# Chunk 1's feature tiles 4 to 7 as seven block products, with chunk 0 run through to its end before chunk 1

## The chip, the cores and the metric

The kernel runs on one core of a Trainium2 chip. The metric is the device time of the whole program in microseconds (us). The time before the change is 263.39 us, the median of three runs (263.13 to 263.56).

## What is computed

An attention block with polynomial sketches is followed by a two-layer network with exact GELU. Cut to what matters:

```python
# q, k, v: (4 batches, 4 heads, 1088 tokens, 32);  S1, S2: (8, 32)
phi(x)[i, j] = (S1 x)[i] * (S2 x)[j]                # 64 features of each token
kv = sum over tokens of phi(k) v^T;  z = sum over tokens of phi(k)
attn = phi(q) kv / (phi(q) z + 1e-6)
x = attn as (4352 tokens, 128)
h = x @ w_in                                         # w_in: 128 x 2048
out = (0.5 * h * (1 + erf(h / sqrt(2)))) @ w_out     # w_out: 2048 x 128
```

The weights arrive as 64-bit numbers. The kernel turns them into 32-bit ones on the chip ("rounding": five instructions on VectorE or GpSimd and two on ScalarE for each piece of weights).

## The kernel before

**Tiling.** The 4352 tokens are cut into eight chunks of 512 tokens (two for each batch) and a ninth for the remainders. The 2048 hidden columns are sixteen feature tiles of 128, called fi. For each chunk n and each fi, `hidden(n, fi)` (matmuls at L683, GELU by ScalarE at L690) computes 128 features by 512 tokens. The result then has to be multiplied by its 128 rows of `w_out` and added up over fi.

**Two ways of the second product.** In the usual way, `project(n, fi)` (L818) is one 128x128 by 512 matmul that adds into one PSUM bank, `o_of[n]`. In the other way, four feature tiles make a block (b = fi // 4), and each pair of them is multiplied as a 2 by 2 block matrix with seven products in place of eight. This needs sums of features, `token_sums(n, b)`: four GpSimd instructions of 128x512 (L732 to L735). It also needs sums of weights, `channel_sums(i)`: four GpSimd instructions (L719 to L722) for weight piece i. A call of `two_products` (L767) issues two products of 64x256 that run side by side in the two column halves of TensorE; a block has seven such calls. They add into two PSUM banks, `acc[n]`, which `drain(n)` (ScalarE L779 to L781, VectorE L783 to L788) and `combine(n)` put together. Where a chunk used both ways, `take_usual(n)` (ScalarE, L795) has copied the usual part out of PSUM, and `combine` adds it.

Before the change, chunks 0 and 1 run fi 0 to 7 in the usual way (`USUAL = 8`) and fi 8 to 15 as blocks 2 and 3. All later chunks run blocks 0 to 3. The last, the ninth, is done in the usual way.

**Order.** Every engine runs its instructions in the order of the program text, and the text is written step by step: step t does `hidden` of entry t of the list `steps`, then everything that `at(t, ...)` has put into slot t, then the second products put into `products[t]`. Before the change, `steps` runs chunk 0 fi 0-3, chunk 1 fi 0-3, chunk 0 fi 4-7, chunk 1 fi 4-7, chunk 0 fi 8-15 (steps 16 to 23), chunk 1 fi 8-15 (steps 24 to 31), and from step 32 the whole of chunk 2, and so on. A usual product stands two steps behind its hidden tile (`LAG = 2`). Seven-product calls stand three to six steps behind the last hidden tile of their block.

**What shares those steps.** The weights lie in five pieces: fi 0-1, 2-3, 4-7, 8-11 and 12-15. `round_at(t, ...)` spreads the rounding of a piece over steps t and t + 1: `w_in_sb[2]` at 4, `w_out_sb[2]` at 6, `w_in_sb[3]` at 8, `w_out_sb[3]` at 10, `w_in_sb[4]` at 12 and `w_out_sb[4]` at 14. The last multiplication of the two pieces 4 is done by GpSimd (L297), the others by VectorE. `channel_sums(3)` is put at step 13 and `widen_v_rem(1)` (L349 and L351, a memset and a copy that reads values brought by DMA) at step 12. Batch 1's keys (`features_of_all`, L934; `outer_of_all`, L942 to L949; `turn_keys_rem`, L333; `add_tokens`, L958; `finish_keys`, L428; `turn_kv`, L458; `z_sum`) fill steps 16 to 23. The factors of chunk 2's queries (`query_sketch`, L568; `query_outer`, L580 to L603) come at step 24. At step 28 VectorE turns batch 2's keys (`key_turn_blocks`, L359). At step 31 TensorE does `sketch_and_attend(3)` (L568, then L617) and `features_of_all(2)` (L934, which reads the turned keys).

Buffers: `hps` (the hidden tiles) has two banks, so that `hidden` of step t waits for the GELU of step t - 2. `ops` has two banks. `block` tiles have three buffers.

Of the kernel before, what the change touches and what calls it, by code (L numbers as in the profile page):

```python
# [16 lines left out]
def kernel(  # L17
# [24 lines left out]
    NF = d_ff // 128  # L42
# [7 lines left out]
    NCH = J // JC  # L50
    C = D + 1
    LAG = 2
    NMAIN = B * NCH
    NB = 4

    USUAL = 8
    NCHUNK = NMAIN + 1
    assert B == 4 and d_model == 128 == H * D == JC * D == 2 * F and H == 4 and REM == 64 and NCH == 2

# [7 lines left out]
    def work_banks():  # L67

        return wps.tile([128, 2, CW], FP, name="w_ps")

    def work_bank():
        return work_banks()[:, 0]

    def halves(banks):
        return [banks[:, i] for i in range(2)]

    def hidden_bank():
        return hps.tile([128, CW], FP, name="h_ps")

    def out_bank():  # L80
        return ops.tile([128, CW], FP, name="o_ps")
# [55 lines left out]
    def block(dtype=U32):  # L137

        b = big.tile([128, NB, 512], U32, name="block", bufs=3)
        return b if dtype == U32 else b.bitcast(dtype)  # L140
# [314 lines left out]
    def turn_kv(b, banks):  # L455

        for rows in (slice(0, 64), slice(64, 128)):
            pe.matmul(banks[rows, 1, :128], lhsT=kv_T[b], rhs=ident, start=True, stop=True)  # L458
        act.copy(out=kz[b], in_=banks[:, 1, :128])
# [200 lines left out]
    def turn_half(n, i, ps, copy):  # L660
        if i == 0:
            xT[n] = att.tile([128, CW], FP, name="xT", bufs=3)
        for j in range(2):
            pe.transpose(ps[:, j * 128:(j + 1) * 128], in_=x_tok[n, i][:, j].rearrange("p h d -> p (h d)"), identity=ident)
        copy(out=xT[n][:, i * 256:(i + 1) * 256], in_=ps[:, :256])
# [4 lines left out]
    def w_tile(w, fi):  # L670
        i = max(i for i, (c0, c1) in enumerate(pieces) if c0 <= fi * 128)
        at = fi * 128 - CUTS[i]
        return w[i][:, at:at + 128]
# [3 lines left out]
    def hidden(n, fi, by_halves=False):  # L677
        W = width[n]
        ps = first_banks.pop((n, fi)) if (n, fi) in first_banks else hidden_bank()
        w = w_tile(w_in_sb, fi)  # L680
        for rows in (slice(0, 64), slice(64, 128)) if by_halves else (slice(0, 128),):
            if (n, fi) not in begun:
                pe.matmul(ps[rows, :W], lhsT=w[:, rows], rhs=xT[n][:, :W], start=True, stop=True)  # L683
        if n < NCH and fi < USUAL:
            g_of[n, fi] = mlp.tile([128, CW], FP, name="g", bufs=4)
        else:
            if fi % NB == 0:
                blocks[n, fi // NB] = block(FP)
            g_of[n, fi] = blocks[n, fi // NB][:, fi % NB]
        act.activation(out=g_of[n, fi][:, :W], in_=ps[:, :W], func=ACT.Gelu)  # L690
# [58 lines left out]
        return sums[n, b][j][:, e], T[j][:, k]  # L749

    def first_block(n):
        return USUAL // NB if n < NCH else 0

    def two_products(n, b, i):

# [37 lines left out]
    def take_usual(n):  # L793
        usual[n] = mlp.tile([128, CW], FP, name="g", bufs=4)
        act.copy(out=usual[n], in_=o_of[n])  # L795
# [9 lines left out]
        return N[:, 1]  # L805

    def project(n, fi, parts=range(B // 2)):
        first, final = fi == 0, fi == (USUAL if n < NCH else NF) - 1
        if first:
            o_of[n] = out_bank() if n < NMAIN else [work_bank() for i in range(B // 2)]  # L810
        g = g_of[n, fi]
        if n == NMAIN:

            for i in parts:
                pe.matmul(o_of[n][i][:, :128], lhsT=g[:, i * 128:(i + 1) * 128], rhs=w_tile(w_out_sb, fi),  # L815
                          start=first, stop=final)
            return
        pe.matmul(o_of[n], lhsT=w_tile(w_out_sb, fi), rhs=g, start=first, stop=final)  # L818
# [65 lines left out]
    late = []  # L884
# [32 lines left out]
    w_out[0].fields()  # L917


    steps = [(n, fi) for f in range(0, USUAL, 4) for n in range(NCH) for fi in range(f, f + 4)]  # L920
    steps += [(n, fi) for n in range(NCHUNK) for fi in range(USUAL if n < NCH else 0, NF)]
    slots = {t: [] for t in range(len(steps) + LAG)}

    def at(t, f, *a):
        slots[t].append(lambda: f(*a))
# [40 lines left out]
    held = {}  # L966
# [21 lines left out]
    def round_at(t, w, product_by=dve):  # L988
        r = []
        at(t, lambda: (r.append(Rounding(w)), r[0].low_words(), r[0].fields()))  # L990
        at(t + 1, lambda: (r[0].exponents(), r[0].mantissas(), r[0].signs(), r[0].product(product_by)))
# [2 lines left out]
        round_at(t0, w_in_sb[i + 2])  # L994
        round_at(t1, w_out_sb[i + 2])
    round_at(12, w_in_sb[4], pool)
    at(13, channel_sums, 3)

    at(12, widen_v_rem, 1)
    for r in range(2):  # L1000
        at(14, key_turn_blocks, 1, r)
    round_at(14, w_out_sb[4], pool)
    at(15, query_turn, 2)
    at(16, features_of_all, 1)
    at(16, outer_of_all, 1)
    at(16, turn_keys_rem, 1)
    at(17, features_rem, 1)
    at(17, add_tokens, 1)
    at(18, channel_sums, 4)

    at(21, finish_keys, 1, False)
    at(22, lambda: turn_kv(1, held["kv"]))
    at(23, z_sum, 1)
    at(23, fold_z, 1)
    at(23, query_turn, 3)
    at(24, query_sketch, 2)
    at(24, query_outer, 2)
    for i, t in enumerate((25, 26, 28)):
        at(t, channel_sums, i)
    at(11, spread_sketches)  # L1020
    at(40, repeat_first_z)
    for n in range(3, NCHUNK):

        t = (n - 1) * NF
# [28 lines left out]
    products = {t: [] for t in range(len(steps) + LAG)}  # L1053
    done = {t: [] for t in range(len(steps) + LAG + 1)}
    drains = {t: [] for t in range(len(steps) + LAG + 1)}
    for t, (n, fi) in enumerate(steps):
        if n < NCH and fi < USUAL:
            products[t + LAG].append((project, n, fi))
            if fi == USUAL - 1:
                slots[t + LAG + 1 + 2 * n].append(lambda n=n: take_usual(n))  # L1060
        elif n == NMAIN:
            at_ = max(t + LAG, (n * NF + 5) if fi < 3 else (n * NF + 6) if fi < 5 else 0)
            if fi < NF - 4:
                products[at_].append((project, n, fi))
            if fi == NF - 1:

                products[at_] += [(project, n, NF - f, (i,)) for f, i in ((4, 0), (3, 0), (2, 0), (4, 1), (1, 0), (3, 1),
                                                                          (2, 1), (1, 1))]
                done[at_ + 1].append(n)
        elif fi % NB == NB - 1:  # L1070
            b = fi // NB
            opens = b == first_block(n)
            late = int(n < NCH or n == NCH and opens)
            for later, pairs in ((3, 3), (4, 2), (5, 2)) if opens else ((2, 2), (3, 2), (4, 1), (5, 2)):
                later += late
                for i in range(pairs):
                    products[t + later].append((two_products, n, b, len([p for q in products.values() for p in q
                                                                        if p[:3] == (two_products, n, b)])))
            if b == NF // NB - 1:
                drains[t + 6 + late].append(n)  # L1080
                done[t + 12].append(n)

    for t in range(len(steps) + LAG):
        if t < 4:

            hidden(0, t)
            if t == 1:
                w_out[0].low_words()
                w_out[0].exponents()
                w_out[0].finish()  # L1090
                w_out[1].fields()
            if t == 2:
                w_out[1].low_words()
            if t == 3:
                banks = work_banks()
                numerators_by_token(1, halves(banks), range(JC))
                w_out[1].mantissas(by_pool=True)
                w_out[1].exponents()
                divide(1, banks, range(JC), by_head_pair=False)
                w_out[1].signs()  # L1100
                w_out[1].product()
                for u in range(4):
                    for f, *a in products[u]:
                        f(*a)
            continue
        if t == 4:
            for i, copy in enumerate((by_act, by_dve)):
                turn_half(1, i, work_bank(), copy)
            first_hidden(1, 0)
            for f, *a in products[t]:  # L1110
                f(*a)
            first_hidden(1, 1)
        for n in drains[t]:
            drain(n)
        if t < len(steps):
            n, fi = steps[t]
            hidden(n, fi, by_halves=t >= 18 and (n < NMAIN or fi < 5))
        if t < len(steps) and steps[t][0] < NMAIN and steps[t][1] % NB == NB - 1:
            n, b = steps[t][0], steps[t][1] // NB
            if b >= first_block(n):  # L1120
                token_sums(n, b)
        for f in slots[t]:
            f()
        for n in done[t]:
            store(n)
        if t != 4:
            for f, *a in products[t]:
                f(*a)
# [41 lines left out]
```

## Time and profile before

| | |
|---|---|
| median of three runs | 263.39 us (263.13 to 263.56) |
| the profiled execution: time | 263.46 us |
| the profiled execution: span | 261.7 us (1.8 us lie around it) |
| TensorE (PE) busy | 256.7 us, 98% of the span |
| VectorE (DVE) busy | 150.7 us, 58% |
| ScalarE (ACT) busy | 116.6 us, 45% |
| GpSimd (POOL) busy | 164.0 us, 63% |
| granted TensorE clock | 1.00 throughout |

The busy shares are means over the span; a page of the profile also divides it into forty slices. PE is full in nearly all slices. POOL is nearly idle from about 23 to 39 us and nearly full from 50 to 75 us; DVE is nearly full from 30 to 55 us. A line of the timeline gives the start and the duration in us, the engine, the line of the kernel, and output <- inputs. On TensorE, one 32-bit matmul stands as two records ("x2"), and the durations of consecutive records overlap, so the distance from start to start tells what a matmul takes from the engine.

### The profile page before, as it was taken

How to read it: one execution, taken by the hardware profiler on the slowest of the kernel's cores; microseconds unless marked ns; L12 is line 12 of the kernel's file. 1: busy time of each engine (PE TensorE's matmuls, PEld its weight loads, DVE VectorE, ACT ScalarE, POOL GpSimd, SP SyncE). 2: the span in 40 equal slices, each digit the busy share in tenths (PEclk: the TensorE clock that was granted, in tenths of full speed). 3: DMA queues.
4: the chain of work that ended last, by engine and by line, in shares of the span. 5: the costliest groups of instructions: out<-in, count | busy, mean ns of one | idle time of the engine just before them, and what ended most of it. 6: DMA issues, size and time to landing. Idle time of an engine off the chain costs nothing.

```text
span 261.7 us, 5752 instructions
## 1 busy us (share of the span) xinstructions
PE 256.7 (98%) x2331; PEld 132.7 (51%) x2331; DVE 150.7 (58%) x307; ACT 116.6 (45%) x227; POOL 164.0 (63%) x173
## 2 busy tenths in 40 slices
PE   8999999999999999999999999999999999999994
PEld 6845444344444454444444454454444444445794
DVE  2885879969697997590267948450646042600240
ACT  4674767532635334533335334533362335334441
POOL 3403007799968767687758766967778676877200
PEclk9999999999999999999999999999999999999999
DMA  6469848831000101002000020010000100010020
GB/s 200 139 200 357 164 107 206 214 81 15 3 0 15 28 4 30 10 3 40 3 0 3 0 33 11 3 30 10 3 0 14 30 4 0 14 28 0 3 40 20
DMA packets 29530, 13.48 MB, mean 52 GB/s; under 512 B 21824, under 2 KB 27712, under 8 KB 29504
## 3 DMA queue, kind: packets, MB, share of 16 engines
q1 hardware_dynamic: 29472, 13.12, 20.5%
q8 instruction: 18, 0.29, 0.5%
q14 instruction: 8, 0.07, 0.1%
q10 hardware_dynamic: 32, 0.00, 0.0%
HBM read 10.88 MB, written 2.23 MB: 50 GB/s over the span
## 4 chain that ended last, share of the span: by engine, by line
PE 96%; DVE 1%; ACT 1%; issue 0%; DVEq 0%
PE h_ps L683 44%; PE o_ps L767 33%; PE o_ps L818 5%; PE w_ps L815 3%; PE w_ps L428 1%; PE w_ps L617 1%; PE w_ps L568 1%; PE w_ps L848 1%; PE h_ps L697 1%; PE o_ps L417 1%; PE h_ps L333 1%; PE w_ps L934 1%; PE w_ps L635 0%; PE w_ps L534 0%; DVE x_tok L656 0%
## 5 line engine op out<-in xcount | busy, mean ns | idle before, releaser
L683 PE MATMUL h_ps<-xT,w_in 128*64 128x512 f32 (+3 forms) x514 | 137.3, 576 | 0.0
L690 ACT ACTIVATE block<-h_ps 128x512 f32<-128x512 f32 (+1 forms) x128 | 73.0, 570 | 120.4 <-PE h_ps L683 114.6
L767 PE MATMUL o_ps<-block,w_out 128*64 128x256 f32 x224 | 57.9, 381 | 0.3 <-DVE sums L788 0.3
L683 PEld LDWEIGHTS h_ps<-xT,w_in 128*64 128x64 f32 (+1 forms) x514 | 41.8, 143 | 29.5 <-issue 11.6
L732 POOL TENSOR_TENSOR bits_low<-block 128x512 f32<-128x512 f32 x28 | 35.6, 1273 | 28.7 <-ACT block L690 28.7
L767 PEld LDWEIGHTS o_ps<-block,w_out 128*64 128x64 f32 x224 | 30.1, 137 | 39.3 <-issue 25.3
L733 POOL TENSOR_TENSOR bits_a<-block 128x512 f32<-128x512 f32 x28 | 35.7, 1276 | 13.4 <-ACT block L690 13.4
L734 POOL TENSOR_TENSOR bits_e<-bits_a,block 128x512 f32<-128x512 f32 x28 | 36.3, 1298 | 2.2
L735 POOL TENSOR_TENSOR bits_m<-block,bits_e 128x512 f32<-128x512 f32 x28 | 35.8, 1279 | 2.2
L767 PE MATMUL o_ps<-bits_low,small 128*64 128x256 f32 x112 | 29.3, 384 | 0.0
L767 PE MATMUL o_ps<-block,small 128*64 128x256 f32 x112 | 29.3, 384 | 0.0
L767 PE MATMUL o_ps<-bits_a,small 128*64 128x256 f32 x112 | 29.1, 383 | 0.0
L783 DVE TENSOR_TENSOR sums<-o_ps,sums 64x512 f32<-64x512 f32 x8 | 5.5, 682 | 41.1 <-ACT sums L780 23.6
L767 PE MATMUL o_ps<-bits_m,w_out 128*64 128x256 f32 x112 | 28.8, 380 | 0.0
L580 DVE STREAM_TRANSPOSE w_ps<-w_ps 128x512 f32<-128x512 f32 (+1 forms) x7 | 4.8, 691 | 38.8 <-PE w_ps L568 27.8
L767 PEld LDWEIGHTS o_ps<-block,small 128*64 128x64 f32 x112 | 14.5, 137 | 18.8 <-issue 9.1
L767 PE MATMUL o_ps<-bits_e,small 128*64 128x256 f32 x112 | 17.2, 385 | 0.0
L818 PE MATMUL o_ps<-g,w_out 128*128 128x512 f32 x32 | 16.4, 598 | 0.0
L767 PEld LDWEIGHTS o_ps<-bits_m,w_out 128*64 128x64 f32 x112 | 15.4, 137 | 0.0
L767 PEld LDWEIGHTS o_ps<-bits_a,small 128*64 128x64 f32 x112 | 14.7, 137 | 0.0
L767 PEld LDWEIGHTS o_ps<-bits_low,small 128*64 128x64 f32 x112 | 14.6, 137 | 0.0
L767 PEld LDWEIGHTS o_ps<-bits_e,small 128*64 128x64 f32 x112 | 7.5, 137 | 10.5 <-issue 9.1
(181 smaller groups left out, 300.6 us busy)
## 6 DMA issues: line engine op xcount, KB each, us to landing
out_dram<-oT SPq DMA_DIRECT2D x26, 64.0 KB, 2.2
block<-in_moe_w_in_dram SPq DMA_DIRECT2D x3, 512.0 KB, 7.4
block<-in_moe_w_out_dram SPq DMA_DIRECT2D x3, 512.0 KB, 12.7
k<-in_k_dram SPq DMA_DIRECT2D x12, 128.0 KB, 3.2
v<-in_v_dram SPq DMA_DIRECT2D x12, 128.0 KB, 3.4
q<-in_q_dram SPq DMA_DIRECT2D x24, 64.0 KB, 2.3
k<-in_k_dram SPq DMA_DIRECT2D x2, 256.0 KB, 2.9
q<-in_q_dram SPq DMA_DIRECT2D x2, 256.0 KB, 4.4
```

Of the source, the lines that this page charges most:

```text
L333: pe.transpose(ps[:, i * 128:(i + 1) * 128], in_=s, identity=ident)
L580: dve.transpose(out=tok, in_=ps[:, :, :H2])
L683: pe.matmul(ps[rows, :W], lhsT=w[:, rows], rhs=xT[n][:, :W], start=True, stop=True)
L690: act.activation(out=g_of[n, fi][:, :W], in_=ps[:, :W], func=ACT.Gelu)
L732: pool.tensor_sub(out=s[3], in0=a11, in1=a21)
L733: pool.tensor_add(out=s[1], in0=a21, in1=a22)
L734: pool.tensor_sub(out=s[2], in0=s[1], in1=a11)
L735: pool.tensor_sub(out=s[4], in0=a12, in1=s[2])
L767: pe.matmul(acc[n][bank][half * 64:(half + 1) * 64, col:col + HW], lhsT=fixed, rhs=moving, start=opens and e == 0 and name in "4715", stop ...
L783: dve.tensor_add(out=C[lo, 1], in0=a1[lo], in1=C[lo, 0])
L815: pe.matmul(o_of[n][i][:, :128], lhsT=g[:, i * 128:(i + 1) * 128], rhs=w_tile(w_out_sb, fi), start=first, stop=final)
L818: pe.matmul(o_of[n], lhsT=w_tile(w_out_sb, fi), rhs=g, start=first, stop=final)
```

## The change

Chunk 1 now runs only fi 0 to 3 in the usual way; its fi 4 to 7 become a block of seven products (block 1), as its blocks 2 and 3 already are. The order of the steps becomes: chunk 0 fi 0-3, chunk 1 fi 0-3, chunk 0 fi 4-15 (steps 8 to 19), chunk 1 fi 4-15 (steps 20 to 31). From step 32 on nothing changes. Chunk 0's usual products for fi 5, 6 and 7 are spread to steps 12, 14 and 16. `channel_sums(2)`, which chunk 1's block 1 needs, moves from step 28 to step 9, and `channel_sums(3)` from step 13 to step 12. Batch 1's keys move by two steps or one, and chunk 2's sketch from step 24 to step 26. `hidden` is written as two column halves from step 17 on, before from step 18.

```diff
-    USUAL = 8
+    USUAL = [8, 4]
...
-        if n < NCH and fi < USUAL:
+        if n < NCH and fi < USUAL[n]:
...
-    steps = [(n, fi) for f in range(0, USUAL, 4) for n in range(NCH) for fi in range(f, f + 4)]
-    steps += [(n, fi) for n in range(NCHUNK) for fi in range(USUAL if n < NCH else 0, NF)]
+    steps = [(n, fi) for n in range(NCH) for fi in range(4)]
+    steps += [(n, fi) for n in range(NCHUNK) for fi in range(4 if n < NCH else 0, NF)]
...
     round_at(12, w_in_sb[4], pool)
-    at(13, channel_sums, 3)
+    at(9, channel_sums, 2)
+    at(12, channel_sums, 3)
 
     at(12, widen_v_rem, 1)
...
-    at(16, features_of_all, 1)
-    at(16, outer_of_all, 1)
-    at(16, turn_keys_rem, 1)
-    at(17, features_rem, 1)
-    at(17, add_tokens, 1)
+    at(18, features_of_all, 1)
+    at(18, outer_of_all, 1)
+    at(18, turn_keys_rem, 1)
+    at(19, features_rem, 1)
+    at(19, add_tokens, 1)
     at(18, channel_sums, 4)
 
-    at(21, finish_keys, 1, False)
-    at(22, lambda: turn_kv(1, held["kv"]))
-    at(23, z_sum, 1)
-    at(23, fold_z, 1)
-    at(23, query_turn, 3)
-    at(24, query_sketch, 2)
-    at(24, query_outer, 2)
-    for i, t in enumerate((25, 26, 28)):
+    at(22, finish_keys, 1, False)
+    at(23, lambda: turn_kv(1, held["kv"]))
+    at(24, z_sum, 1)
+    at(24, fold_z, 1)
+    at(24, query_turn, 3)
+    at(26, query_sketch, 2)
+    at(26, query_outer, 2)
+    for i, t in enumerate((25, 26)):
         at(t, channel_sums, i)
...
-        if n < NCH and fi < USUAL:
-            products[t + LAG].append((project, n, fi))
-            if fi == USUAL - 1:
-                slots[t + LAG + 1 + 2 * n].append(lambda n=n: take_usual(n))
+        if n < NCH and fi < USUAL[n]:
+            to = t + LAG + max(fi - NB, 0)
+            products[to].append((project, n, fi))
+            if fi == USUAL[n] - 1:
+                slots[to + 1 + 2 * n].append(lambda n=n: take_usual(n))
...
-            late = int(n < NCH or n == NCH and opens)
+            late = int(n < NCH or n == NCH and opens) + int(n == 0 and opens)
...
-            hidden(n, fi, by_halves=t >= 18 and (n < NMAIN or fi < 5))
+            hidden(n, fi, by_halves=t >= 17 and (n < NMAIN or fi < 5))
```

(`USUAL` becomes `USUAL[n]` also in `first_block` and `project`.)

More of the change, by code (lines that the diff above doesn't have):

```diff
@@ L751, in first_block @@
     def first_block(n):
-        return USUAL // NB if n < NCH else 0
+        return USUAL[n] // NB if n < NCH else 0
     def two_products(n, b, i):
@@ L807, in project @@
     def project(n, fi, parts=range(B // 2)):
-        first, final = fi == 0, fi == (USUAL if n < NCH else NF) - 1
+        first, final = fi == 0, fi == (USUAL[n] if n < NCH else NF) - 1
         if first:
```

## The prediction

> **What bounds the kernel now.** I read the page's busy shares first, then its chain, then the engines' timelines over the stretch that the change reorders.
>
> ```profile
> PE 256.7 (98%) x2331; PEld 132.7 (51%) x2331; DVE 150.7 (58%) x307; ACT 116.6 (45%) x227; POOL 164.0 (63%) x173
> ...
> PE 96%; DVE 1%; ACT 1%; issue 0%; DVEq 0%
> ```
>
> TensorE is busy for 98% of the span and is 96% of the chain that ended last. Work taken from TensorE shortens the run, and whatever makes it wait lengthens it by the full wait, because nothing later has room to take it up. TensorE's timeline gives the two prices, from start to start:
>
> ```profile
> 39.05 1.02 PE L818 MATMUL o_ps<-g,w_out 128*128 128x512 f32 x2
> 39.90 1.02 PE L683 MATMUL h_ps<-xT,w_in 128*128 128x512 f32 x2
> ...
> 77.78 0.38 PE L767 MATMUL o_ps<-block,w_out 128*64 128x256 f32 x1
> 77.79 0.38 PE L767 MATMUL o_ps<-bits_a,small 128*64 128x256 f32 x1
> ...
> 78.65 1.03 PE L683 MATMUL h_ps<-xT,w_in 128*64 128x512 f32 x4
> ```
>
> A usual product takes 39.90 - 39.05 = 0.86, and so does a hidden tile. Two calls of `two_products` stand between 77.78 and 78.65 (each call is two passes of two records), so a call takes 0.43. In the reordered stretch TensorE runs at this pace without a gap. GpSimd and VectorE do not:
>
> ```profile
> 39.31 0.77 POOL L351 COPY v_rem_aug<-v_rem 64x128 f32<-64x128 f32 x1 [16.12 <-DMA v_rem<-in_v_dram]
> 41.26 1.28 POOL L297 TENSOR_TENSOR w_in<-bits_m,bits_e 128x512 f32<-128x512 f32 x1 [1.17 <-DVE bits_e L292]
> 42.49 0.66 POOL L719 TENSOR_TENSOR small<-w_out 128x128 f32<-128x128 f32 x1
> ...
> 44.69 0.78 POOL L722 TENSOR_TENSOR small<-w_out,small 128x128 f32<-128x128 f32 x1
> 45.44 1.26 POOL L297 TENSOR_TENSOR w_out<-bits_m,bits_e 128x512 f32<-128x512 f32 x1
> 46.78 0.46 POOL L719 TENSOR_TENSOR small<-w_out 128x128 f32<-128x128 f32 x1
> ```
>
> ```profile
> 37.77 0.69 DVE L297 TENSOR_TENSOR w_out<-bits_m,bits_e 128x512 f32<-128x512 f32 x1
> 38.38 0.42 DVE L268 TENSOR_SCALAR bits_e<-block 128x512 uint32<-128x512 uint32 x1
> ...
> 40.48 0.69 DVE L292 SCALAR_TENSOR_TENSOR bits_e<-block,bits_r 128x512 uint32<-128x512 uint32 x1 [0.55 <-ACT bits_r L279]
> ```
>
> The reader is to see when `w_in_sb[4]`, the weights of fi 12 to 15, is finished: GpSimd multiplies it from 41.26 to 42.5. Before, its first reader is `hidden` of step 20, near 49.7, seven us later. `channel_sums(3)` comes after it, at 42.49, and takes 2.95 (to 45.44) beside VectorE's rounding; the next four of the same size take 1.8 (46.78 to 48.59).
>
> **What the Trainium skill says.** Perfetto Trace Analysis, section Identifying the Most-Contended Engine, warns that matmul busy time is no good measure of the distance from the peak[...]. The trace agrees (records of 1.02 that start 0.86 apart), so I use start-to-start distances. SBUF — State Buffer, section Who interferes with whom: a VectorE instruction with two SBUF inputs, or in a two-port mode, contends with GpSimd reads. The trace agrees: L719 took 0.66 and 0.46. TensorE: Matmul & The Clock Gate, section Architectural detail, calls GpSimd's queue strictly first in, first out. The trace agrees: behind L351, which sat 16.12 for a DMA, nothing else ran.
>
> **The change part by part.**
>
> *Work.* Four usual products leave (4 x 0.86 = 3.44), seven calls come (7 x 0.43 = 3.01): -0.43 on TensorE. Four token sums are added on GpSimd (4 x about 1.28 = 5.1); GpSimd's backlog from 50 us is dealt with below. ScalarE has the same number of GELUs and copies, VectorE and all DMA issues are the same; SP's queue does not change, so `v_rem` still lands at 39.3.
>
> *The deadline of `w_in_sb[4]`.* Up to step 11 nothing moves on TensorE (its hidden tile starts at 34.75 in both orders). Afterwards chunk 0's products are thinned out: steps 11, 13 and 15 have a hidden tile alone, steps 12 and 14 also a usual product. So steps 11 to 15 hold five hidden tiles and two usual products, 7 x 0.86 = 6.01, and step 16 comes at 40.76. It is now chunk 0's fi 12: the first reader of `w_in_sb[4]`.
>
> *When `w_in_sb[4]` is ready.* Its rounding keeps its steps. But in GpSimd's queue `channel_sums(3)` now stands ahead of `widen_v_rem(1)` and of the multiplication. It needs `w_out_sb[3]`, which VectorE finishes at 37.77 + 0.69 = 38.46, held there by ScalarE's work on step 11, which is not moved. Handing over takes 0.09 (40.48 + 0.69 = 41.17 to 41.26). Then:
> - `channel_sums(3)` from 38.55, beside the same four rounding instructions of VectorE (L268 from 38.38) as in the row above, so 2.95: to 41.50;
> - memset and copy of L349/L351, 0.17 plus between 0.29 and 0.77 (the shortest and the longest copy in the trace), I take 0.6: to 42.1;
> - the multiplication, 1.23 from start to start: to 43.33.
>
> VectorE's own part (L292) is done near 41, so GpSimd decides. TensorE waits at step 16 from 40.76 to 43.35: **+2.6**. Behind it in TensorE's queue stand the usual product of fi 7 and everything else; there is no other work it could do. Bounds: if the sums are not slowed (1.8) and the copy takes 0.29, 42.1 and a wait of 1.3; with the long copy and 0.2 for handing over, 3.0.
>
> *`w_in_sb[3]` for step 12.* Needed at 35.61; VectorE finished it at 34.34 + 0.69 = 35.03. `channel_sums(2)` now runs beside it (from 31.7). It may slip by 0.3, which the 0.58 covers; a slip beyond that is swallowed by the wait at step 16, which ends at a time set by GpSimd.
>
> *The second squeeze: steps 26 to 31.* Before, chunk 2's query factors ran on VectorE before the first drain, at steps 24 to 28. Now the drain of chunk 0 comes at step 26 in front of them, and batch 2's key turns stand behind both. From the trace:
>
> ```profile
> 63.40 1.25 DVE L603 STREAM_TRANSPOSE q_pT<-q_f 128x1024 f32<-128x1024 f32 x1
> 64.57 1.26 DVE L359 STREAM_TRANSPOSE kT<-k 128x512 f32<-128x512 f32 x2
> 68.12 0.68 DVE L783 TENSOR_TENSOR sums<-o_ps,sums 64x512 f32<-64x512 f32 x1 [2.29 <-ACT sums L780]
> ...
> 71.03 0.71 DVE L580 STREAM_TRANSPOSE w_ps<-w_ps 128x512 f32<-128x512 f32 x1
> ```
>
> Counted from the end of chunk 0's last product (67.14 in the trace), VectorE starts the drain after 0.98, has 2.91 of it (68.12 to 71.03), then 6.34 for L580 to L603 (58.23 to 64.57), then 1.26 for the two key turns: 11.5. TensorE, from the same point: six hidden tiles (5.16), L568 twice and L617 (about 0.6, 0.45 and 0.43), nine calls (3.87) and about 0.25 where the shape changes: 10.75 to L934. Its first half needs the first turn (10.9), its second half the second (11.55 with the handover), instead of 10.75 + 0.28: **+0.55**. Bounds: 0 if VectorE is 0.5 faster, 1.0 if it is as much slower.
>
> *Other places.* GpSimd after 43.3: sums of block 2 of chunk 0 to 48.5, `w_out_sb[4]` to 49.8, `channel_sums(4)` to 51.6, block 3 to 56.8, chunk 1's block 1 to 62.2, two small channel sums to 64.7, block 2 to 70. TensorE asks for the first sums of these blocks (1.3 after each block's start, the last at its end) from 49.8, 55.8, 64.5 and 70.1: each is there at least 1.5 ahead. I cost them at nothing; if GpSimd were 3 later, these would be the next stall. The PSUM banks for block 2 of chunk 0 (step 20) are freed by `take_usual` at steps 12 and 17; nothing. The hidden tiles that follow each other directly need the GELU two steps back; ScalarE, with a rounding instruction of 0.7 in each step, has it 0.1 to 0.9 ahead; nothing.
>
> **Sum:** -0.43 + 2.6 + 0.55 = +2.7 against 263.46, so 266.2 for a profiled execution; the median of the runs lies 0.07 lower: **266.1**.
>
> **The rivals.**
> - *Both waits as worked out*, 265.5 to 266.8: chance 0.62.
> - *One of them is much smaller*: GpSimd's sums unslowed (wait 1.3), or the second squeeze absent. -0.43 + 1.3 + (0 to 0.55) gives 264.3 to 265.4. [...]0.20.
> - *GpSimd's backlog spreads*: its sums after 43.3 take 1.6 as the worst row (L734) in the trace, and blocks 3 and 1 arrive late: 1 to 2 more, 267 to 268. 0.08.
> - *The other side: GpSimd is not late.* The mechanism is the deadline at step 16: if the multiplication ends by 40.8, the first wait is nothing, and the work saved remains, with the end of TensorE's ScalarE-bound stretch (four hidden tiles took 3.73 between 47.94 and 51.67, 0.29 over 4 x 0.86): -0.43 - 0.29 = 262.7. It decides when the two waits together fall below 0.43. Against it: `channel_sums(3)` cannot start before 38.46. 0.07; about the same time, 0.03.
> - That the seven products are not made in place of the four: TensorE's instructions in program order hold 14 matmuls of 64x256 more and 4 of 128x512 fewer, so no.
>
> **How the numbers follow.** The likeliest case gives 266.1. From 264.4 to 267.2 holds most of the first case's bounds and of the second's and leaves the faster case and the longest backlog outside. A difference below 0.2% (0.5 us) is about what a measurement of this kernel cannot tell from none. Faster 0.07, same 0.03, slower 0.90.
>
> **What would show it.** Right: in the changed kernel TensorE has a gap of 2 to 3 us before the first hidden tile of fi 12 (chunk 0), released by GpSimd's L297, with L719 to L722 just ahead of that on GpSimd; L934 of batch 2 stands broken into two halves waiting for L359; otherwise the distances 0.86 and 0.43 stay. Wrong: no gap there, or a gap released by something else (ScalarE's GELU, a DMA, `token_sums`), or a span below 263.

## The result, and the profile after

The changed kernel takes 267.85 us, median of five runs (267.63 to 268.36), beside 263.56 for the kernel before, run together with it (263.13 to 265.31). The ratio is 1.016, with an interval from 1.0137 to 1.0183. The kernel became slower, as predicted, but by 4.3 us where 2.7 was predicted, and 267.85 lies above the range (264.4 to 267.2). Single runs of several kernels lie about 1.7 us or more above the others without a lower clock, for no cause found here (265.24 of the kernel before in a later group; 272.52 of the kernel called "both" below, left out of its row), so medians are compared.

The profiled execution took 268.16 (span 266.4), 4.70 more than that of before. These are its busy shares, the granted TensorE clock in the forty slices, the chain's shares by engine, and its group of hidden tiles:

```profile
PE 259.3 (97%) x2353; PEld 133.5 (50%) x2353; DVE 155.2 (58%) x307; ACT 116.3 (44%) x227; POOL 171.5 (64%) x177
...
PEclk9999997999999999999999999999999999999999
...
PE 94%; POOL 2%; DVE 1%; ACT 1%; issue 0%; POOLq 0%
...
L683 PE MATMUL h_ps<-xT,w_in 128*64 128x512 f32 (+3 forms) x516 | 138.5, 578 | 2.3 <-POOL w_in L297 2.3
```

GpSimd (POOL) has entered the chain with 2%, and the hidden tiles have an idle time of 2.3 that GpSimd's L297 ends: the forecast stall. But there is also a 7 in the clock line, in the seventh slice (40 to 46.6 us). The timeline of TensorE shows both:

```profile
40.04 1.02 PE L683 MATMUL h_ps<-xT,w_in 128*128 128x512 f32 x2
43.36 2.08 PE L683 MATMUL h_ps<-xT,w_in 128*128 128x512 f32 x2 [2.29 <-POOL w_in L297]
45.23 1.80 PE L818 MATMUL o_ps<-g,w_out 128*128 128x512 f32 x2
46.95 1.94 PE L683 MATMUL h_ps<-xT,w_in 128*64 128x512 f32 x8
```

Step 16 would have started at 40.04 + 0.86 = 40.90 and starts at 43.36: a wait of 2.46. The hidden tile after it takes 45.23 - 43.36 = 1.87, and the usual product 46.95 - 45.23 = 1.72, twice the usual 0.86. The table of stretches (length; busy times of PE, PEld, DVE, ACT, POOL; granted clock; DMA share; GB/s) gives the reason:

```profile
40.00:43.36 3.36, 1.06 (x4) 0.19 (x2) 3.36 (x5) 1.43 (x3) 3.22 (x6) 1.00 1.00 236
43.36:46.77 3.41, 3.41 (x4) 1.17 (x4) 3.41 (x2) 0.64 (x2) 3.33 (x3) 0.50 0.61 164
46.77:49.00 2.23, 2.23 (x17) 0.67 (x24) 2.10 (x2) 1.49 (x4) 1.74 (x2) 1.00 0.93 247
```

From the end of the wait the granted clock was 0.50 for 3.41 us. GpSimd's queue ahead of the wait stands as worked out, and goes on behind it without a pause of more than 0.1:

```profile
38.69 0.57 POOL L719 TENSOR_TENSOR small<-w_out 128x128 f32<-128x128 f32 x1 [0.71 <-DVE w_out L297]
...
40.80 0.79 POOL L722 TENSOR_TENSOR small<-w_out,small 128x128 f32<-128x128 f32 x1
41.52 0.21 POOL L349 MEMSET v_rem_aug<- 128x128 f32 x1
41.80 0.28 POOL L351 COPY v_rem_aug<-v_rem 64x128 f32<-64x128 f32 x1
42.05 1.26 POOL L297 TENSOR_TENSOR w_in<-bits_m,bits_e 128x512 f32<-128x512 f32 x1
43.27 1.26 POOL L732 TENSOR_TENSOR bits_low<-block 128x512 f32<-128x512 f32 x1
44.49 1.25 POOL L733 TENSOR_TENSOR bits_a<-block 128x512 f32<-128x512 f32 x1
45.83 1.34 POOL L734 TENSOR_TENSOR bits_e<-bits_a,block 128x512 f32<-128x512 f32 x1
```

Beside it, VectorE's timeline shows something the prediction did not have:

```profile
42.41 3.62 DVE L268 TENSOR_SCALAR bits_e<-block 128x512 uint32<-128x512 uint32 x1
45.95 1.50 DVE L273 TENSOR_SCALAR bits_a<-block 128x512 uint32<-128x512 uint32 x1
```

and ScalarE's timeline what follows from it:

```profile
46.13 0.72 ACT L279 ACTIVATE bits_r<-bits_e,below 128x512 uint32<-128x512 uint32 x1 [4.43 <-DVE bits_e L268]
46.76 0.58 ACT L690 ACTIVATE block<-h_ps 128x512 f32<-128x512 f32 x1
```

L268, the first instruction of the rounding of `w_out_sb[4]`, took 3.62. Before the change the same instruction took 0.52, and others of its kind 0.42:

```profile
42.31 0.52 DVE L268 TENSOR_SCALAR bits_e<-block 128x512 uint32<-128x512 uint32 x1
```

ScalarE's L279 reads its output. ScalarE runs in the order of the text, so the GELU of step 16 stood behind L279 until 46.76, and step 18 of TensorE needs that GELU. I call this the held GELU. In this execution, with TensorE at half clock, step 18 did not have to stop for it (steps 17 and 18 follow each other from 46.95). The second squeeze came as forecast; TensorE's timeline before and after:

```profile
68.96 0.66 PE L568 MATMUL w_ps<-qT,S_abc 64*32 64x256 f32 x16
69.41 0.64 PE L617 MATMUL w_ps<-q_pT,kz 64*32 64x256 f32 x16
69.84 0.64 PE L934 MATMUL w_ps<-kT,S_ab 64*32 64x256 f32 x16
70.41 0.43 PE L767 MATMUL o_ps<-block,small 128*64 128x256 f32 x1
```


```profile
74.08 0.66 PE L568 MATMUL w_ps<-qT,S_abc 64*32 64x256 f32 x16
74.54 0.67 PE L617 MATMUL w_ps<-q_pT,kz 64*32 64x256 f32 x16
75.13 1.23 PE L934 MATMUL w_ps<-kT,S_ab 64*32 64x256 f32 x16
76.29 0.43 PE L767 MATMUL o_ps<-block,w_out 128*64 128x256 f32 x1
```

From L568 to the first call is 76.29 - 74.08 = 2.21; before it was 70.41 - 68.96 = 1.45. The squeeze costs 0.76.

The whole difference of the two profiled executions, in order of time:

| | us | predicted |
|---|---|---|
| later at step 15 | 0.14 | 0 |
| seven calls for four usual products | -0.43 | -0.43 |
| wait of step 16 for L297 | 2.46 | 2.6 |
| hidden tile 1.87 and product 1.72 instead of 0.86 each | 1.87 | nothing |
| second squeeze | 0.76 | 0.55 |
| L333 and L399, now ahead of a hidden tile in halves, take 0.26 and 0.37 to the next start (before, ahead of a usual product, 0.17 and 0.16) | 0.30 | nothing |
| a wait of before, of L767 for a drain's L788, is gone | -0.3 | not seen |
| sum (measured: 4.70) | 4.80 | 2.7 |

So the sum fails mainly at one place, the 1.87 after the wait. About 1.7 of it is the clock: at full clock the same two take 0.96 and 0.95, as the experiments show.

### The profile page after: what moved, and what is told of

It is laid out like the page before. It is cut to its first block, busy times and chain, and to the rows that moved or that the text cites. A ratio compares the mean times of both kernels' runs of the same rounds, so it can differ in the third digit from the quotient of the medians.

```text
span 266.4 us, 5799 instructions
## 1 busy us (share of the span) xinstructions
PE 259.3 (97%) x2353; PEld 133.5 (50%) x2353; DVE 155.2 (58%) x307; ACT 116.3 (44%) x227; POOL 171.5 (64%) x177
## 4 chain that ended last, share of the span: by engine, by line
PE 94%; POOL 2%; DVE 1%; ACT 1%; issue 0%; POOLq 0%
PE h_ps L683 43%; PE o_ps L767 34%; PE o_ps L818 4%; PE w_ps L815 3%; PE w_ps L428 1%; PE w_ps L617 1%; PE w_ps L568 1%; PE w_ps L848 1%; PE h_ps L697 1%; PE w_ps L934 1%; PE o_ps L417 1%; PE h_ps L333 1%; POOL w_in L297 0%; PE w_ps L635 0%; PE w_ps L534 0%
## 5 line engine op out<-in xcount | busy, mean ns | idle before, releaser
L690 ACT ACTIVATE block<-h_ps 128x512 f32<-128x512 f32 (+1 forms) x132 | 75.4, 571 | 122.5 <-PE h_ps L683 115.5
L767 PE MATMUL o_ps<-block,w_out 128*64 128x256 f32 x232 | 59.9, 381 | 0.0
L732 POOL TENSOR_TENSOR bits_low<-block 128x512 f32<-128x512 f32 x29 | 36.9, 1274 | 29.2 <-ACT block L690 29.2
L767 PEld LDWEIGHTS o_ps<-block,w_out 128*64 128x64 f32 x232 | 31.0, 137 | 39.3 <-issue 25.2
L733 POOL TENSOR_TENSOR bits_a<-block 128x512 f32<-128x512 f32 x29 | 37.2, 1282 | 14.7 <-ACT block L690 14.7
L734 POOL TENSOR_TENSOR bits_e<-bits_a,block 128x512 f32<-128x512 f32 x29 | 37.7, 1299 | 2.3
L735 POOL TENSOR_TENSOR bits_m<-block,bits_e 128x512 f32<-128x512 f32 x29 | 37.2, 1284 | 2.3
L767 PE MATMUL o_ps<-block,small 128*64 128x256 f32 x116 | 30.2, 383 | 0.0
L767 PE MATMUL o_ps<-bits_low,small 128*64 128x256 f32 x116 | 30.2, 383 | 0.0
L767 PE MATMUL o_ps<-bits_a,small 128*64 128x256 f32 x116 | 30.1, 382 | 0.0
L767 PE MATMUL o_ps<-bits_m,w_out 128*64 128x256 f32 x116 | 29.8, 379 | 0.0
L767 PEld LDWEIGHTS o_ps<-block,small 128*64 128x64 f32 x116 | 15.2, 137 | 19.8 <-issue 10.3
L767 PE MATMUL o_ps<-bits_e,small 128*64 128x256 f32 x116 | 17.8, 385 | 0.0
L767 PEld LDWEIGHTS o_ps<-bits_m,w_out 128*64 128x64 f32 x116 | 15.8, 137 | 0.0
L767 PEld LDWEIGHTS o_ps<-bits_low,small 128*64 128x64 f32 x116 | 15.2, 137 | 0.0
L767 PEld LDWEIGHTS o_ps<-bits_a,small 128*64 128x64 f32 x116 | 15.2, 137 | 0.0
L767 PEld LDWEIGHTS o_ps<-bits_e,small 128*64 128x64 f32 x116 | 7.7, 136 | 10.6 <-issue 8.8
L818 PE MATMUL o_ps<-g,w_out 128*128 128x512 f32 x24 | 13.0, 631 | 0.0
```

Of the source, the lines that this page charges most:

```text
L732: pool.tensor_sub(out=s[3], in0=a11, in1=a21)
L733: pool.tensor_add(out=s[1], in0=a21, in1=a22)
L734: pool.tensor_sub(out=s[2], in0=s[1], in1=a11)
L735: pool.tensor_sub(out=s[4], in0=a12, in1=s[2])
L767: pe.matmul(acc[n][bank][half * 64:(half + 1) * 64, col:col + HW], lhsT=fixed, rhs=moving, start=opens and e == 0 and name in "4715", stop ...
```

## The experiments

Three theories for the extra time. **The clock**: a pause of 2.5 on TensorE halves its clock, and that costs what the profile shows, about 1.9. **The held GELU**: L268 cannot get in beside GpSimd, and TensorE would stop at step 18 even at full clock. **Neither**: something in the new order that was not seen yet. The kernel before ran beside each group of kernels, with a median between 263.5 and 263.6.

### The sums behind the multiplication again

```diff
-    at(12, channel_sums, 3)
+    at(13, channel_sums, 3)
```

> channel_sums(3) goes back to step 13, behind the multiplication of w_in_sb[4] on GpSimd; all else as changed. Theory (queue order): the multiplication starts at about 40.6 instead of 42.05 and ends near 41.9, so TensorE's wait at step 16 shrinks from 2.46 to about 1.0, and the time by 1.5 or more: 266.3 or less, and down to 264.9 if the halved clock that follows the wait goes with it. Rival (VectorE's own part of the rounding decides): the wait stays above 2 and the time above 267.3.

Measured 265.30 (264.72 to 267.04), ratio to before 1.0064 (1.0045 to 1.0083). TensorE's timeline:

```profile
39.91 1.02 PE L683 MATMUL h_ps<-xT,w_in 128*128 128x512 f32 x2
42.05 1.12 PE L683 MATMUL h_ps<-xT,w_in 128*128 128x512 f32 x2 [1.11 <-POOL w_in L297]
43.01 1.02 PE L818 MATMUL o_ps<-g,w_out 128*128 128x512 f32 x2
```

One step number is worth 267.85 - 265.30 = 2.55. The wait is 42.05 - 40.77 = 1.28, 1.2 less; the multiplication starts at 40.72, now decided by VectorE's L292. The other 1.35 is what came after the wait: the tile behind it takes 0.96, the clock of this profile is 1.00 throughout, and L268 took 0.50. So the place in GpSimd's queue is the cause, directly and by what follows. The clock and the held GELU are not yet apart.

### The wait filled, the first fields earlier, and both

Three kernels, run together. The first lets TensorE multiply zeros during the wait, so that its clock has no reason to fall. The second starts the rounding of `w_out_sb[4]` earlier (L268 and L273 at step 13), ahead of GpSimd's multiplication, so that the GELU is not held by L268. The third does both.

```diff
+        if t == 16:
+            keep_busy(5, work_bank())
         if t < len(steps):
```

```diff
-    round_at(14, w_out_sb[4], pool)
+    ahead = []
+    at(13, lambda: (ahead.append(Rounding(w_out_sb[4])), ahead[0].fields()))
...
+    at(14, lambda: ahead[0].low_words())
+    at(15, lambda: (ahead[0].exponents(), ahead[0].mantissas(), ahead[0].signs(), ahead[0].product(pool)))
```

> Five matmuls of noughts (128x256, 0.43 each, 2.15 in all) stand ahead of step 16's hidden tile, so that TensorE is busy while it would wait. Theory (clock): the 3.4 us at half clock after the wait, in which a hidden tile and a usual product took 1.87 and 1.72, are gone, the clock is 1.00 in every run, and up to 1.9 is saved: 266.0. Rival (port and ScalarE): the GELU of step 16 is still held until 46.8 behind the rounding of w_out_sb[4], TensorE stops for it instead at step 18, and only 0.2 to 0.6 is saved: 267.3 to 267.7.

> The two VectorE instructions that open the rounding of w_out_sb[4] (L268, L273) stand at step 13, ahead of batch 1's key turns, so that L268 is not issued while GpSimd runs three instructions without a gap. Theory (port): L268 takes under 0.7 instead of 3.62, ScalarE's L279 comes before 43, the GELU of step 16 follows its hidden tile directly. If the clock is still halved after the wait, the time changes by under 0.3 (267.6 to 268.0), because TensorE is then the slower of the two; runs at full clock would come to about 266.5. Rival (no port effect): L268 takes over 2 at its new place as well.

> Both: five matmuls of noughts ahead of step 16's hidden tile, and the opening of the rounding of w_out_sb[4] at step 13. If the clock and the held GELU are two covers for the same loss, each hiding the other, this saves what neither saves alone: about 1.9, to 266.0, with the wait at step 16 itself (2.46) and the one at L934 (0.57) still in it. If the two are independent, it saves the sum of what e2 and e4 save.

| | us, median (lowest to highest) | ratio to before | granted clock in its runs |
|---|---|---|---|
| filled | 267.57 (267.25 to 268.06) | 1.0138 (1.0111 to 1.0166) | 0.998 to 1.0 |
| fields earlier | 267.49 (266.40 to 268.72) | 1.0136 (1.0097 to 1.0176) | three at 0.998 to 1.0, three at 0.991 to 0.993 |
| both | 266.93 (266.68 to 267.00) | 1.0111 (1.0082 to 1.014) | 1.0 |

The median of the second hides two groups. Its runs at full clock took 266.40, 266.53 and 266.56; those at 0.991 to 0.993 took 268.43, 268.65 and 268.72. A clock halved for 3.41 us lowers the mean over 266 by 3.41 x 0.5 / 266 = 0.006, so I take this for the half clock, present in some executions of one kernel and absent in others; the changed kernel's 3.41 us are the only ones seen in a trace. The five runs of the changed kernel fall apart too, but less in time: 267.63, 267.69 and 267.85 at 0.997 to 1.0 (runs of the kernel before also go down to 0.997), and 268.16 and 268.36 at 0.991 and 0.992.

What decides it can be worked out from the traces. In each of the eleven, the entries of the record of the granted clock begin whole multiples of 3.413 us apart (in the changed kernel's at 5.81, 43.36, 46.77 and 265.23: 43.36 - 5.81 = 37.55 = 11 x 3.413). Cut into such stretches, the changed kernel's pause (41.06 to 43.36) falls into a single one, 39.95 to 43.36, which has 2.29 without a matmul. In the three profiled runs with a pause of 2.3 to 2.7 and a full clock, an edge cuts the pause: the stretch with most of it has 1.97 (fields earlier), and 1.67 and 1.52 in two kernels of the sections below. The end of each run, where TensorE has no more work, fits too. In all, the clock fell to half twelve times in the eleven traces, each time after a stretch with 2.28 idle or more, and never after one with 1.97 or less. So what counts is the idle part of one stretch, with a limit between 1.97 and 2.28, and a pause of 2.3 halves the clock only if it happens to fall whole into one. No run set the position of a pause on purpose.

The filled kernel shows the held GELU alone, in TensorE's timeline:

```profile
40.75 2.34 PE L848 MATMUL w_ps<-const-float32-0.0 128*128 128x256 f32 x10
43.21 1.13 PE L683 MATMUL h_ps<-xT,w_in 128*128 128x512 f32 x2
44.17 1.02 PE L818 MATMUL o_ps<-g,w_out 128*128 128x512 f32 x2
45.13 1.08 PE L683 MATMUL h_ps<-xT,w_in 128*64 128x512 f32 x4
47.24 1.08 PE L683 MATMUL h_ps<-xT,w_in 128*64 128x512 f32 x4 [1.04 <-ACT block L690]
```

The tiles run at full pace, and then step 18 stops for 1.04 because the GELU of step 16 is late (it starts at 46.61). In the kernel with early fields, at full clock, that stop is gone:

```profile
43.43 1.12 PE L683 MATMUL h_ps<-xT,w_in 128*128 128x512 f32 x2 [2.65 <-POOL w_in L297]
44.40 1.02 PE L818 MATMUL o_ps<-g,w_out 128*128 128x512 f32 x2
45.35 1.94 PE L683 MATMUL h_ps<-xT,w_in 128*64 128x512 f32 x8
```

Here the eight records of steps 17 and 18 follow each other, and the GELU of step 16 started at 44.59. The runs sorted by both causes (medians, or the mean of two; the changed kernel ran earlier, beside a before of 263.56, the others beside 263.58):

| | GELU held | GELU not held |
|---|---|---|
| clock full | 267.69 (changed), 267.57 (filled) | 266.53 (early), 266.93 (both) |
| clock halved | 268.26 (changed) | 268.65 (early) |

The half clock alone costs 268.65 - 266.53 = 2.1, the held GELU alone 267.69 - 266.53 = 1.2 (between the two filled kernels 0.6), and both together 268.26 - 266.53 = 1.7. The comparison is not clean. In the two kernels with early fields the wait at step 16 is 43.43 - 39.76 - 0.86 = 2.81, 0.35 longer, since GpSimd's memset and copy, now beside the moved L268 and L273, took 0.87 instead of 0.53. That is why both causes together look cheaper than the half clock alone, whose 2.1 is also more than the 1.7 that 3.41 at half speed takes from a full TensorE (an estimate); no run of that kind was profiled. The traces give cleaner prices. From the start of step 15 to L934 TensorE takes 8.78 with both causes (changed), 8.36 with the held GELU alone (filled), and 7.14 with the same wait and almost none of either (the kernel of the next section). So the held GELU costs 1.2 and both together 1.6.

They cover each other: a TensorE at half speed does not reach step 18 before the late GELU is ready. Both theories are right, and either cause alone accounts for more than half of the observed time. That is why filling the wait gained nothing that these runs can tell (267.57 beside 267.85, as its rival said), although it removed the half clock, which none of the eleven runs of "filled" and "both" in the table has. With early fields the runs at half clock took 268.4 to 268.7 where 267.6 to 268.0 was expected, and "both" took 266.93 where 266.0 was expected; of each miss the longer wait explains 0.35, and the rest is open. The third theory falls: with both causes gone the kernel stands 266.53 - 263.58 = 3.0 above before ("both": 3.4), and 2.7 was predicted; the longer wait fits the difference.

### How L268 gets in

In the changed kernel L268 started while GpSimd's multiplication ran (42.41) and ended at 46.03, 0.2 after GpSimd's first pause (45.74 to 45.83, ahead of L734, which needs L733's result). If VectorE is shut out until GpSimd pauses, moving the pause forward by one instruction must shorten L268 by one instruction, 1.2. In the sums of chunk 0's block 2 alone, the first of the four, on which no other depends, is put third:

```diff
-        pool.tensor_sub(out=s[3], in0=a11, in1=a21)
+        if (n, b) != (0, 2):
+            pool.tensor_sub(out=s[3], in0=a11, in1=a21)
...
+        if (n, b) == (0, 2):
+            pool.tensor_sub(out=s[3], in0=a11, in1=a21)
```

> As changed, but in the sums of block 2 of chunk 0 GpSimd does the sum that the next one depends on first (order of the four: 2, 3, 1, 4), so that after the multiplication of w_in_sb[4] it runs two instructions without a gap, then a pause of about 0.1 for its own result, instead of three and then a pause. Theory (VectorE's L268 is let in only in a pause of GpSimd): L268, issued near 42.4, takes about 2.3 instead of 3.62, and the GELU of step 16 comes about 1.3 earlier. Rival (it is slowed by GpSimd's load as such): about 3.6 as before.

One run, 266.14 at full clock. The line numbers of the sums are other here: L734 and L735 are the second and third sum, which were L733 and L734. VectorE's and GpSimd's timelines:

```profile
42.06 2.40 DVE L268 TENSOR_SCALAR bits_e<-block 128x512 uint32<-128x512 uint32 x1
```

```profile
41.70 1.26 POOL L297 TENSOR_TENSOR w_in<-bits_m,bits_e 128x512 f32<-128x512 f32 x1
42.92 1.26 POOL L734 TENSOR_TENSOR bits_a<-block 128x512 f32<-128x512 f32 x1
44.26 1.34 POOL L735 TENSOR_TENSOR bits_e<-bits_a,block 128x512 f32<-128x512 f32 x1
```

L268 is shorter by 1.22, one GpSimd instruction, and again ends 0.2 after GpSimd's pause (44.18 to 44.26). Among these block sums the pause decides, as far as one run of each kernel shows it. Early fields do not end the contention either: there VectorE's L287, 0.69 otherwise, takes 2.97 (43.41 to 46.38) across GpSimd's pause at 45.82, but no GELU stands behind it. The pause is not the whole rule: with the sums behind the multiplication, L268 (41.78) came in where L297 ended and L719 began without a pause, in 0.50. What makes these two neighbours different stays open.

### The second squeeze removed

```diff
-                at(t - 3 if n > 3 else t - 4, key_turn_blocks, b, r)
+                at(t - 3 if n > 3 else 25, key_turn_blocks, b, r)
```

> As changed, but VectorE turns batch 2's keys (L359) at step 25, ahead of chunk 0's drain, and no longer at step 28 behind chunk 2's query factors. Theory (second squeeze): L934 at step 31 no longer waits for L359 and takes 0.59 instead of 1.16, but the query factors end 1.26 later unless VectorE is idle at step 25 (it was, 1.56 before L783), so 0.5 to 0.6 is saved: 267.3 against 267.85. Rival: VectorE has no room, L617 waits instead for L603, and nothing is saved.

Measured 266.95 (266.50 to 267.62), ratio 1.0129 (1.0103 to 1.0156). TensorE's timeline in the profiled run:

```profile
73.17 0.66 PE L568 MATMUL w_ps<-qT,S_abc 64*32 64x256 f32 x16
73.63 0.67 PE L617 MATMUL w_ps<-q_pT,kz 64*32 64x256 f32 x16
74.08 0.64 PE L934 MATMUL w_ps<-kT,S_ab 64*32 64x256 f32 x16
74.66 0.43 PE L767 MATMUL o_ps<-block,w_out 128*64 128x256 f32 x1
```

74.66 - 73.17 = 1.49, as before the change (1.45). The saving in this stretch is 0.72, and 0.9 between the medians, more than the 0.5 to 0.6 expected. The key turns were the cause. This profiled run had the full clock (two of the five, 267.56 and 267.62, have means of 0.993 and 0.994), and TensorE's list of waits (us in total, times, longest) has the two stalls of step 16 and step 18 one beside the other:

```profile
PE h_ps L683 <- POOL w_in L297: 2.3, 1, 2.3
PE h_ps L683 <- ACT block L690: 1.0, 1, 1.0
```

### Can the seven products pay?

Three kernels give `w_in_sb[4]` the earlier place (`w_out_sb[3]` the later one). The first does only this, with `channel_sums(3)` at step 13. The second also leaves all multiplications to VectorE, starts `w_out_sb[4]` at step 15 and turns the keys at step 25. The third moves `finish_keys` and `turn_kv` of batch 1 on by one step as well.

```diff
-        round_at(t1, w_out_sb[i + 2])
-    round_at(12, w_in_sb[4], pool)
+        round_at(t1, (w_out_sb[2], w_in_sb[4])[i])
+    round_at(12, w_out_sb[3], pool)
...
-    at(12, channel_sums, 3)
+    at(13, channel_sums, 3)
```

The second has `round_at(12, w_out_sb[3])` there, the key turns as in the experiment before, and

```diff
-    round_at(14, w_out_sb[4], pool)
+    round_at(15, w_out_sb[4])
```

The third has all this and

```diff
-    at(22, finish_keys, 1, False)
-    at(23, lambda: turn_kv(1, held["kv"]))
+    at(23, finish_keys, 1, False)
+    at(24, lambda: turn_kv(1, held["kv"]))
```

> As changed, but the rounding of w_in_sb[4] stands at steps 10 and 11 (multiplication by VectorE) and that of w_out_sb[3] at 12 and 13 (multiplication by GpSimd, then channel_sums(3) at step 13). Theory (deadline of w_in_sb[4]): it is ready near 38.5, TensorE has no wait at step 16, no halved clock. Against that GpSimd's sums of block 2 of chunk 0 come later (channel_sums(3) to about 45.5, sums to 50.7) and TensorE stops for them at step 20 and for block 3 at step 22, by 1.2 and 0.5: -0.43 + 0.57 + 1.7 gives 265.3. Rival (the held GELU was the cause, not the deadline): a time above 266.5.

> All of it: w_in_sb[4] rounded at steps 10 and 11, w_out_sb[3] at 12 and 13 and w_out_sb[4] at 15 and 16, all multiplied by VectorE; channel_sums(3) at step 13; batch 2's key turns at step 25. If the waits at step 16 and at L934, the held GELU and the halved clock are all that stands between the changed kernel and its work, what is left is -0.43 for the seven products, plus up to 0.5 for the third call of step 20, which asks for GpSimd's third sum near 48.2 and gets it near 48.6: 263.0 to 263.6, beside 263.5 of before. Rival (another wait takes their place): above 264.5.

> As e8_all, but batch 1's sum over tokens (L428) stands at step 23 and its turn (L458) at step 24, one step later each. In e8_all that sum was the one place where TensorE waited (0.91, for VectorE's L404, itself late because the rounding of w_out_sb[4] took 1.14, 1.75 and 1.64 beside GpSimd in place of 0.69 each). Theory (that wait is all that is left): it goes, and the time is 0.9 below e8_all's 264.18, 263.3, which is the -0.43 of the seven products, less some small change, beside 263.5 of before: no difference that can be told, or 0.2 to 0.4 faster. Rival (a new wait, for the turn or for z): 263.8 or more.

Measured 264.81 (ratio 1.0041, 1.0027 to 1.0056), 264.18 (1.0019, 1.0005 to 1.0032) and 264.61 (1.005, 1.0028 to 1.0072). In none of them does TensorE wait at step 16, and none beats the kernel before. None took what was expected: the first was better (the waits of 1.2 and 0.5 for GpSimd's sums are not in TensorE's list), the second and third were worse and have a new wait each. TensorE's list of waits has in the second

```profile
PE w_ps L428 <- DVE k_p_rem L404: 0.9, 1, 0.9
```

and in the third

```profile
PE w_ps L428 <- ACT kz L459: 0.7, 1, 0.7
```

In the second kernel the rounding on VectorE (L292 took 1.75 and L297 1.64 beside GpSimd, 0.69 each alone) pushes batch 1's keys back, and L428 waits for them. In the third, L428 is late enough, but its second use (`z_sum`) then follows `turn_kv` too closely. The second kernel's span without its wait is 262.1 - 0.9 = 261.2, 0.5 below the 261.7 of before; by the medians it is 264.18 - 0.9 = 263.3, 0.2 below. The work itself can be read from the same traces: added up from start to start over the whole run, L818 takes 14.00 before and 10.50 in the second kernel, L767 86.06 and 89.09, together 0.47 less. That the total falls by as much was worked out and not run: I found no order that has the seven products and no new wait. The first kernel lies 1.3 above before where -0.43 and 0.76 explain 0.3. Of the rest, 0.6 lies in its seven-product calls (L767 takes 12.01 from start to start up to step 33, and 11.38 in the second kernel, for as many calls); in the profiled run (264.39, where before took 263.46) these three account for the difference, and the 0.4 that is left between the medians was not located. Seven products in the old order of the steps were not tried: `ops` has two banks, and that order would hold more partial sums at a time.

## Why the prediction was right and wrong

- **The work, -0.43**: right in the traces (-0.47 on L818 and L767), not shown in a total time.
- **The wait for `w_in_sb[4]`, 2.6**: right in place, cause and size. The multiplication began at 42.05 (42.1 was worked out) and TensorE at 43.36 (43.35); that both agree to 0.05 is in part luck, since TensorE's step 15 and GpSimd's queue both began 0.14 late and GpSimd made it up (its four sums took 2.83 and not 2.95). The wait is 2.46, also in the traces where step 15 came earlier. One step number gave back 1.2 of it.
- **The step that failed** is "ScalarE, with a rounding instruction of 0.7 in each step, has it 0.1 to 0.9 ahead; nothing". It priced ScalarE's own work and not what that work waits for. ScalarE's L279 waits for L268, and L268 now met a GpSimd queue packed together: four sums, memset, copy, multiplication and then, at once, the block sums. The prediction used this contention for GpSimd's side (2.95 in place of 1.8), and did not ask what the same pair of ports does to VectorE. In the Trainium skill, SBUF — State Buffer, section Who interferes with whom, says that in a two-port mode whoever issues first has the pair for the whole instruction and the other fully blocks; it counts `tensor_scalar`, which L268 is, among the instructions that can run so, and no run here shows the mode itself. The trace agrees with the blocking and goes further: L268 took 3.62 against 0.52 before, having stayed out during the GpSimd instruction that ran and the two after it. Cost: 1.2 alone.
- **A second omission** is the price of the wait. It was entered at its own length. In some runs a pause of this length also halves the clock for 3.41, which costs 0.4 beside the held GELU (8.78 against 8.36) and 2.1 where the GELU is not held. In the Trainium skill, TensorE: Matmul & The Clock Gate, section What's actually happening, gives a half clock after an idle window of about 3.4 us, and says that the window runs freely, so that its edge falls differently from run to run. The length of 3.41 agrees, and so does that some runs have it and some not. But the page asks for an idle window, and the pauses here were 2.3 to 2.7 long; the measurement decides: 2.28 idle within one stretch of 3.413 was enough, 1.97 was not.
- **The second squeeze, 0.55**: right in cause, mis-sized by 0.2: it measured 0.76. Some 0.14 of it shows ahead of L934, whose first record starts 0.59 after L617's, 0.45 where the turns come early.
- **The rivals.** "GpSimd is not late" and "one of them is much smaller" are refuted by the 2.46 and 0.76. "GpSimd's backlog spreads" (267 to 268) has the right time for a wrong reason: no wait for GpSimd's later sums is in TensorE's list. The forecast was right on the sign and on the two waits, and its range was too narrow by the two effects that follow a stall.

## What to carry to other kernels

A step number moves a place in four queues at once, and an instruction placed ahead of another on a busy engine is a promise that its result can wait; read the first reader's time before moving. Price a new wait with what comes after it: the clock that may fall, and the instruction that a newly packed queue shuts out on another engine. Two such costs can cover each other, so that taking away one shows little; try both together before calling either harmless.

## What was not expected of the hardware

- A VectorE instruction that waits beside GpSimd need not get the next turn. L268 stayed out during three consecutive GpSimd instructions and came in at a pause of about 0.1, in which GpSimd waited for its own result (3.62, and 2.40 with the pause one instruction earlier).
- By the mean clock of the runs, a pause of 2.3 to 2.7 on TensorE halved its clock in two of five runs of the changed kernel, three of six with early fields and two of five with early key turns; a pause of 1.1 did so in none of fifteen. The traces say which: the clock halves for 3.413 us when one of the stretches of 3.413, counted from a start that differs from run to run, has 2.28 or more without a matmul, not when it has 1.97.
